# Eight accumulating transfers from GpSimd's queue in the fourth batch of a pooled attention with a mixture of experts

## Chip, cores and metric

One core of a Trainium2 chip runs the whole program. The metric is the device time of one execution in microseconds; less is better.

## What is computed

Attention with pooled queries over 8 batches of 8 heads, then a mixture of experts in which each row goes to one of 8 experts. Cut to what matters here:

```python
# q, k, v: (8, 8, 1152, 64) float32
q_pool = q.reshape(B, H, S // 2, 2, D).mean(axis=3)
scores = scale * np.matmul(q_pool, k.transpose(0, 1, 3, 2))
scores = scores - np.max(scores, axis=-1, keepdims=True)
attn = np.exp(scores)
attn = attn / (np.sum(attn, axis=-1, keepdims=True) + 1e-09)
x = np.matmul(attn, v)                      # -> (4608, 512)
# each row of x: the expert of the largest logit, relu(x @ w1[e]) @ w2[e], times its weight
```

## The kernel before

**Tiling.** The attention goes batch by batch (`b` from 0 to 7), in a batch by pairs of heads (`hp` from 0 to 3), and in a pair by halves of the 576 pooled queries (`half`, 288 each). Such a half of a pair is called a half pair below; there are 64 of them, counted from 0, and 24 to 31 are the fourth batch (`b == 3`). The transposed scores of a half pair fill one score tile `s` of 128 partitions by 9 chunks by 2 heads by 288 queries, that is 5184 floats in each partition. There are four such tiles (`UNITS`), so half pair 33 takes the tile that 29 had.

**What is done with a half pair.** `scores` lets TensorE multiply keys and queries chunk by chunk into a PSUM bank (L631). VectorE scales each chunk into `s` and takes its minimum (L635), nine of these "takes" a half pair. Then a bound for the exponential is spread to all partitions (L656, L662), and ScalarE overwrites `s` with exponentials in five pieces (L666). `chunk_sum` lets GpSimd add the nine chunks up: a first fold of chunks 0 to 2 with 3 to 5 and a second that adds 6 to 8 (both 1728 floats a partition), and a third of 576 (all L726), into a tile `fold` of which there are three; TensorE adds up the partitions of the folds of both halves (L716). In the last half pair of a batch only the first fold is made (L722), and TensorE does the rest (L709). `values` multiplies `s` with the value tile (L770), nine steps a half pair, about ten microseconds after the exponentials.

**GpSimd's other work in a batch.** It adds neighbouring queries before their transposition (`qp`, L520, four a batch), which VectorE then turns (`qT`, L533), and it issues six scatters into the lists of the experts (L951).

**The order** of each engine's instructions is fixed before the run. `Flow.add` takes each step with an engine, an estimated time, a key (a due time; lower goes first) and what it waits for; `Flow.emit` plays the steps through with these estimates and puts each engine's instructions in the order in which the play started them. `Flow.carry` adds a step that issues a transfer, and behind it a step on a pretended engine (`DMA2` where GpSimd issues) for the transfer's own time. A step holds the tiles in its `holds` from the first step that names a tile to the last, in the play and on the chip. The play's figures that matter here are these:

```python
LATE = dict(PE=250, DVE=130, ACT=130, POOL=60, SP=100, DMA=1700, DMA2=1700, REST=0)
return s and self.add("DMA2" if eng == "POOL" else "DMA", move, lambda: None, key, [s], holds, late=late + (1200 if eng == "POOL" else 0))
def pool(n):
    return 140 + 2.125 * n
```

GpSimd executes in order: an instruction that waits holds up all behind it.

Of the kernel before, what the change touches and what calls it, by code (L numbers as in the profile page):

```python
# [9 lines left out]
F32 = mybir.dt.float32  # L10
# [4 lines left out]
ALU = mybir.AluOpType  # L15
# [22 lines left out]
K_SUM = 25  # L38
# [12 lines left out]
RAW = 6  # L51
XT = 2
LI_BUFS = 6
RE_BUFS = 8
LEAD = 100
AHEAD = 190
XR2 = 4
XR = 6
Y_BUFS = 2
# [204 lines left out]
def kernel(  # L264
# [10 lines left out]
    nc = tc.nc  # L275
# [4 lines left out]
    P = 128  # L280
# [7 lines left out]
    NFC = DF // P  # L288
# [128 lines left out]
    class Pools:  # L417
        h = last = None
# [20 lines left out]
    def act(n):  # L439
        return 110 + 0.833 * n  # L440

    def dve(n):
        return 67 + 1.042 * n
# [12 lines left out]
    def hold_of(kind, make):  # L456
        h = Hold(kind, lambda: make(h))
        return h
# [7 lines left out]
    def score_banks(o):  # L466
        return hold_of("st", lambda h: o.ps_s.tile([P, 2, 512], F32, **h.own("st")))

    def value_banks(o):
        return hold_of("pa", lambda h: o.ps_m.tile([P, 2, 512], F32, **h.own("pa", 1)))  # L470

    def done(*steps):
        return [s for s in steps if s is not None]
# [219 lines left out]
    def every(steps):  # L693
        return [*{id(s): s for s in steps if s is not None}.values()]
# [62 lines left out]
    def values(o, f, key, x, s, ready, hp, half, xT):  # L757
        pa = value_banks(o)
        key += K_AV
        to = slice(half * HQ, (half + 1) * HQ)  # L760
        p = None
        for c in range(NC):
            mark = Pools()

            def product(c=c, mark=mark):

                for i in range(2):
                    for h in range(2):
                        up, cs = slice(i * D, (i + 1) * D), slice(h * D, (h + 1) * D)
                        mark.made = nc.tensor.matmul(pa.t[cs, i, :HQ], x.vn.t[up, h, c, :], s.t[up, c, h],  # L770
                                                     start=c == 0, stop=c == NC - 1, tile_position=(up.start, cs.start))

            p = f.add("PE", 485, product, key + 20.0 * c / NC, done(p, x.v, ready[c]), [pa, x.vn, s], QUADS)
            mark.step = p
            o.marks.append(mark)
        a = f.add("ACT", act(HQ) - 44, lambda: nc.scalar.copy(xT.t[:, hp, to], pa.t[:, 0, :HQ]), key + 20 + K_FREE, done(p), [pa, xT])
        return f.add("DVE", 100 + dve(HQ), lambda: nc.vector.tensor_tensor(  # L777
            xT.t[:, hp, to], xT.t[:, hp, to], pa.t[:, 1, :HQ], ALU.add), key + 20 + K_FREE, done(p, a), [pa, xT])
# [25 lines left out]
    def attend(o, f, key, b, hp, xT, sm, summed):  # L804
        x = load_pair(o, f, key, b, hp)
        outs = []
        end = not o.exact and hp == NHP - 1 and b == B - 1
        for half in range(2):
            at = key + 20 * half
            s, r = scores(o, f, at, x, half, EXPS)  # L810
            summed += chunk_sum(o, f, at + 20, s, r, b, hp, half, sm, summed[-1:])
            outs.append(values(o, f, at + 10 - (40 if end and half else 0), x, s, r, hp, half, xT))
        return done(*outs)

# [401 lines left out]
    def add_raw(m, cm, reuse):  # L1216
        m.r = cm.enter_context(tc.tile_pool(name="mr", bufs=RAW, reuse_waits=reuse))

    def add_moe(m, cm, reuse, **side):
        m.x = cm.enter_context(tc.tile_pool(name="mx", bufs=1, reuse_waits=reuse, **side))  # L1220
        m.w = cm.enter_context(tc.tile_pool(name="mw", bufs=1, reuse_waits=reuse, **side))
        m.w1 = [cm.enter_context(tc.tile_pool(name=f"mw1{j}", bufs=1, reuse_waits=reuse, **side)) for j in range(4)]
        m.ps = cm.enter_context(tc.tile_pool(name="mps", bufs=2, space=PSUM, reuse_waits=reuse))
# [182 lines left out]
    with ExitStack() as cm, ExitStack() as units, ExitStack() as pairs:  # L1406
        o, m = open_attention(False, cm, pairs, units), Pools()
        m.stored = []

        def swap_units():  # L1410
            units.close()
            add_moe(m, units, "tile", side="right")

        f = Flow(dict(st=S_BUFS, s=UNITS, qn=1, vn=3, kp=2, qp=1, kT=KT_BUFS, qT=KT_BUFS,
                      fold=FOLD_BUFS, pa=1, sm=2, xT=2, rec=2, row=ROW_BUFS, lw=1, ex=1, de=1,
                      ohb=1, di=2, re=2, rec2=RE_BUFS, li=LI_BUFS, ix=LI_BUFS, xr=XR, xq=XR2, xt=XT, raw=RAW, x=1, x0=1, **{f"{w}{j}": 1 for w in ("w1", "w2") for j in range(4)}, **{f"h{c}": 1 for c in range(NFC)}, ph=2, py=2, px=2, y=Y_BUFS),
                 ("vn", "fold", "s", "st"), ("x", "xt", "xq", *(f"{w}{j}" for w in ("w1", "w2") for j in range(4)), *(f"h{c}" for c in range(NFC)), "ph", "py", "px", "y"), swap_units)
        hold = []
        pw = score_banks(o)

        def warm_up():
            for i in range(WARM):
                nc.tensor.matmul(pw.t[:, 0], ones, ones.unsqueeze(1).broadcast_to([P, 4, P]), start=True, stop=True)

        if WARM:
            f.add("PE", 2900 * WARM, warm_up, -1000, holds=[pw])
        for b in range(B):
            xT = tile_of(o, "xT", [P, NHP, NQ])
            rec = tile_of(o, "rec", [QP, 2, 3, H])
            sm = tile_of(o, "sm", [P, HQ], bufs=1)  # L1430
            outs, summed = [], []
            for hp in range(NHP):
                outs += attend(o, f, PAIR * (b * NHP + hp), b, hp, xT, sm, summed)
                if b == hp == 0:
                    o.gate = f.carry("SP", 2700, gate_weights, 60, outs, [], 900)
                    f.carry("SP", 960, empty_lists, 1, outs, [], 900)
                    f.carry("SP", 2000, last_rows, 100, outs, [], 3400)
            key = PAIR * (b * NHP + NHP)
            outs.append(row_sums(o, f, key, sm, done(*summed), rec, b == B - 1))
            if b == B - 1:  # L1440
                for x in first:
                    x.rows = x.rows()
                    hold += x.rows
            outs = routing(o, f, key, b, xT, rec, outs, hold)
            if b == B - 2:
                hold, first = first_slots(o, m, f, key + K_FIRST, outs)


        def swap_pairs():
            pairs.close()  # L1450
            add_raw(m, pairs, "tile")
            m.x0 = pairs.enter_context(tc.tile_pool(name="mx0", bufs=1, reuse_waits="tile"))

        raw_here = done(f.add("SP", 10, swap_pairs, key - 1000, o.turned))
        table = slot_table(o, f, key + K_SLOT + K_TAB, outs[:1])
        flag(o, f, key + K_SLOT + 20, [*outs, *table])
        order = [(early, i, TW) for i in range(EARLY)] + [(wide, i, TW) for i in range(WIDE)]
        order += [((etab, rtab), i, T) for i in range(STATIC_SLOTS)]
        base, marks = key + K_SLOT, []
        for i, (tab, s, n) in enumerate(order):  # L1460
            at = base + SLOT * i
            experts, places_ = tab if isinstance(tab, tuple) else (tab[:, 0], tab[:, 1])
            if tab is early:
                x = first[s]
                known = done(x.found)
            else:
                x = tokens_of(o, f, at - AHEAD, places_, s, n, table, outs, m=m, steps=marks[i - 2],
                              used=PLACES[s] if tab is wide else BU)
                known = table
            weights_of(m, f, x, at - 200 if i else at - 1000, experts, s, [*known, *raw_here])  # L1470
            turn_tokens(o, m, f, x, at - (110 if i == 0 else 50), i == 0, raw_here)
            x.w1, x.w1_ready = split_weights(m, f, x, "w1", at - 40, 8, 0)
            first_products(o, m, f, x, at)
            x.w2, x.w2_ready = split_weights(m, f, x, "w2", at, 10, 0)
            second_products(o, m, f, x, at + 50)
            marks.append(() if f.room is None or i < 2 else x.marks)
        f.add("POOL", 2500, lambda: nc.gpsimd.drain(), at - AHEAD + 4, x.rows)
        f.emit()
        by_hand.close()
# [4 lines left out]
    with tc.If(more > 0):  # L1484
        again = nc.values_load(stab[0:1, 1:2], min_val=0, max_val=1,
                               skip_runtime_bounds_check_because="a comparison's result")
        with tc.If(again > 0):
            reset_state()
            empty_lists()
            with ExitStack() as cm:  # L1490
                o = open_attention(True, cm, cm, cm)
                with tc.For_i(0, B, 1) as b:
                    f = Flow()
# [14 lines left out]
        with ExitStack() as cm:  # L1508
            o, m, f = Pools(), Pools(), Flow()
# [5 lines left out]
            with tc.For_i(first, last, 1) as s:  # L1515
                x = tokens_of(o, f, 0, rtab, s, T, (), ())
# [34 lines left out]
```

## Time and profile before

| | us |
|---|---|
| median of 3 runs | 1131.37 (1130.13 to 1131.44) |
| the profiled execution, whole | 1125.42 |
| its span, first instruction to last | 1123.6 |
| attention in it, roughly | 0 to 660 |
| mixture of experts in it, roughly | 660 to 1123.6 |

In what follows PE is TensorE's matmul, PEld its weight load, DVE VectorE, ACT ScalarE, POOL GpSimd and SP SyncE. Times within the program count from the start of the span.

### The profile page before, as it was taken

The page shows a single profiled execution, that of the slowest core. Times are in us where ns is not written, and L with a number is a line of the kernel's source. Part 1 is how long each engine was busy: PE and PEld are TensorE (multiplying, and loading weights), DVE is VectorE, ACT ScalarE, POOL GpSimd, SP SyncE. Part 2 cuts the span into 40 slices and gives each one's busy share as a digit, 9 for nine tenths or more (in the row PEclk, how much of TensorE's full clock was granted, in tenths as well). Part 3 has the DMA queues.
Part 4 walks back from the last instruction along what each step waited for, and adds up shares of the span by engine and source line. Part 5 has one row for each costly group of instructions (what it writes and reads, how often), then busy time and mean ns, then how long its engine had stood idle before and what let it go on. Part 6 is the DMA issues. An engine that isn't in the chain of part 4 may idle for free.

```text
span 1123.6 us, 32966 instructions
## 1 busy us (share of the span) xinstructions
PE 1109.8 (99%) x13317; PEld 797.1 (71%) x13317; DVE 875.9 (78%) x2244; ACT 619.7 (55%) x835; POOL 857.6 (76%) x488
## 2 busy tenths in 40 slices
PE   9999999999999999999999999999999999999997
PEld 5565565565565565655655558998889989899996
DVE  7898998988989979989989969755555665677761
ACT  3756565666556656566557465544444445555551
POOL 3899999999999899998999854576666655456511
PEclk9999999999999999999999999999999999999999
DMA  9876757537738738637635159865555666577640
GB/s 158 141 139 111 129 86 124 113 66 122 115 66 132 112 64 139 114 66 134 112 63 99 27 169 243 232 188 166 164 174 176 201 192 191 191 233 255 229 158 30
DMA packets 387502, 158.06 MB, mean 141 GB/s; under 512 B 302694, under 2 KB 357762, under 8 KB 387342
## 3 DMA queue, kind: packets, MB, share of 16 engines
q1 hardware_dynamic: 376718, 134.91, 54.4%
q0 software_dynamic: 10464, 20.78, 5.9%
q8 instruction: 106, 1.74, 0.8%
q14 instruction: 54, 0.44, 0.2%
q10 hardware_dynamic: 160, 0.20, 0.1%
HBM read 135.02 MB, written 22.07 MB: 140 GB/s over the span
## 4 chain that ended last, share of the span: by engine, by line
PE 66%; DVE 15%; issue 6%; POOL 5%; DMA 4%; SPq 2%; ACT 0%; POOLq 0%; DVEq 0%; ACTq 0%
PE py L1384 17%; PE ph L1354 16%; PE pa L770 15%; PE st L631 14%; DVE s L635 8%; POOL fold L726 3%; DMA vn<-in_v_dram 2%; SPq L490 2%; DVE kT L529 2%; PE st L716 2%; DVE row L937 1%; PE st L709 1%; POOL qp L520 1%; DVE qT L533 1%; DMA x_runs<-row 1%
## 5 line engine op out<-in xcount | busy, mean ns | idle before, releaser
L666 ACT ACTIVATE s<-s,bias 128x1152 f32<-128x1152 f32 (+1 forms) x320 | 351.3, 1152 | 166.4 <-DVE bias L662 156.7
L635 DVE TENSOR_SCALAR_CACHE_REDUCE s<-st 128x576 f32<-128x576 f32 x576 | 415.1, 748 | 32.4 <-PE st L631 21.7
L631 PE MATMUL st<-qT,kT 64*64 64x288 f32 x4608 | 359.9, 407 | 4.6 <-DVE s L635 2.8
L770 PE MATMUL pa<-s,vn 64*64 64x288 f32 x4608 | 351.4, 404 | 1.0 <-DVE xT L777 0.8
L631 PEld LDWEIGHTS st<-qT,kT 64*64 64x64 f32 x4608 | 166.9, 133 | 121.3 <-DVE s L635 37.3
L770 PEld LDWEIGHTS pa<-s,vn 64*64 64x64 f32 x4608 | 174.6, 133 | 104.3 <-DVE xT L777 10.8
L726 POOL TENSOR_TENSOR fold<-s 128x1728 f32<-128x1728 f32 x55 | 213.0, 3875 | 5.5 <-ACT s L666 3.1
L726 POOL TENSOR_TENSOR fold<-fold,s 128x1728 f32<-128x1728 f32 x55 | 213.0, 3876 | 0.9
L1354 PE MATMUL ph<-xh,w1h 128*128 128x248 f32 (+4 forms) x512 | 155.6, 304 | 0.2 <-DVE hl L1364 0.2
L1354 PE MATMUL ph<-xh,w1l 128*128 128x248 f32 (+4 forms) x512 | 154.6, 302 | 0.0
L1354 PE MATMUL ph<-xl,w1h 128*128 128x248 f32 (+4 forms) x512 | 154.6, 302 | 0.0
L1226 DVE TENSOR_TENSOR w2l<-raw,w2h 128x1024 fp32r<-128x1024 f32 x64 | 78.3, 1223 | 80.6 <-ACT w2h L1311 76.8
L1083 POOL DMA_INDIRECT xr<-x_runs,ix x76 | 97.5, 1283 | 51.6 <-issue 26.0
L1384 PE MATMUL py<-w2h,hh 128*128 128x512 f32 x328 | 128.1, 391 | 0.0
L1384 PE MATMUL py<-w2h,hl 128*128 128x512 f32 x328 | 127.8, 390 | 0.0
L1384 PE MATMUL py<-w2l,hh 128*128 128x512 f32 x328 | 127.8, 390 | 0.0
L1393 POOL DMA_INDIRECT out_dram<-y,rec x41 | 43.9, 1071 | 85.7 <-ACT y L1401 70.3
L1362 ACT ACTIVATE hh<-ph 128x372 fp32r<-128x372 f32 (+4 forms) x100 | 49.3, 493 | 108.2 <-PE ph L1354 108.0
L1354 PEld LDWEIGHTS ph<-xh,w1h 128*128 128x128 f32 x512 | 96.4, 188 | 2.6 <-issue 0.9
L1354 PEld LDWEIGHTS ph<-xl,w1h 128*128 128x128 f32 x512 | 96.4, 188 | 0.7
L1354 PEld LDWEIGHTS ph<-xh,w1l 128*128 128x128 f32 x512 | 96.4, 188 | 0.0
L1364 DVE SCALAR_TENSOR_TENSOR hl<-ph,hh 128x372 fp32r<-128x372 f32 (+4 forms) x100 | 55.6, 556 | 51.1 <-ACT hh L1362 50.8
(230 smaller groups left out, 1339.1 us busy)
## 6 DMA issues: line engine op xcount, KB each, us to landing
raw<-in_moe_w_dram SPq DMA_DIRECT2D x128, 512.0 KB
kp<-in_k_dram SPq DMA_DIRECT2D x124, 144.0 KB
vn<-in_v_dram SPq DMA_DIRECT2D x124, 144.0 KB
qn<-in_q_dram SPq DMA_DIRECT2D x120, 144.0 KB
x_runs<-row SPq DMA_DIRECT2D x96, 99.0 KB
xr<-x_runs,ix POOLq DMA_INDIRECT x76, 4.3
x_runs<-empty SPq DMA_DIRECT2D x4, 297.0 KB
xq<-x_runs,ix POOLq DMA_INDIRECT x52, 3.3
```

What stands on the lines that cost most here:

```text
L631: nc.tensor.matmul(pt.t[to, h, :HQ], x.kT.t[up, c * P + i * D:c * P + (i + 1) * D], x.qT.t[up, cols], start=True, stop=True, tile_position ...
L635: nc.vector.tensor_scalar(s.t[:, c], pt.t[:, :, :HQ], -SCALE, None, op0=ALU.mult, op1=ALU.min, accum_out=mx.t[:, c:c + 1],)
L666: nc.scalar.activation(s.t[:, c0:c0 + n], s.t[:, c0:c0 + n], AF.Exp, bias=bias.t, scale=-1.0)
L726: add = lambda to, a, b: nc.gpsimd.tensor_tensor(to, a, b, ALU.add)
L770: mark.made = nc.tensor.matmul(pa.t[cs, i, :HQ], x.vn.t[up, h, c, :], s.t[up, c, h], start=c == 0, stop=c == NC - 1, tile_position=(up.sta ...
L1083: ins = nc.gpsimd.indirect_dma_start(out=x.xr[i // NQD].t[:, i % NQD, :], out_offset=None, in_=xg, in_offset=bass.IndirectOffsetOnAxis(ap= ...
L1226: (nc.gpsimd if eng == "POOL" else nc.vector).tensor_tensor(lo, raw, hi.bitcast(F32), ALU.subtract)
L1354: mark.made = nc.tensor.matmul(view()[:, i, :], a[:, c, fp], b[:, c, :n], start=c == 0 and k == 0, stop=c == NDC - 1 and k == 2)
L1362: a = f.add("ACT", act(nb * n) - 44, lambda home=home, apart=apart: nc.scalar.activation(home(0), apart(), AF.Relu), at - 20, done(p), [ph ...
L1364: d = f.add("DVE", dve(nb * n), lambda home=home, apart=apart: nc.vector.scalar_tensor_tensor(home(1), apart(), 0.0, home(0).bitcast(F32), ...
L1384: mark.made = nc.tensor.matmul(py.t, blocks(a)[:, c * x.nr + r], b[:, c % 2, :], start=c == 0 and k == 0, stop=c == NFC - 1 and k == 2)
L1393: ins = nc.gpsimd.indirect_dma_start(out=out, out_offset=bass.IndirectOffsetOnAxis(ap=x.re.t.bitcast(I32)[:, r, 0:1], axis=0), in_=y.t, in ...
```

## The change

A tile `probe` of 128 partitions by 1728 floats is added, and GpSimd sets it to zero once, at the start. In the fourth batch each half pair gets one more step on GpSimd: a transfer that adds the last `n` floats of each partition of the score tile, after the exponentials, onto the first `n` of `probe`. `n` is 1728 for both halves of the first two pairs, 1152 for those of the third and 576 for those of the fourth: 864, 864, 576 and 288 KB a transfer. Nothing reads `probe`. Each transfer waits for the exponentials of its half pair and for the landing of the transfer before it, holds the score tile, and enters the play with 1200 ns for its issue and 6000 ns for its move. Its key is that of the half pair's folds.

```diff
             summed += chunk_sum(o, f, at + 20, s, r, b, hp, half, sm, summed[-1:])
+            if not o.exact and b == 3:
+                n = (1728, 1728, 1152, 576)[hp]
+                o.joined = f.carry("POOL", 1200, lambda n=n, s=s: o.join(n, s), at + 20 + K_SUM, done(o.joined, *every(r)), [s, o.onto], 6000)
             outs.append(values(o, f, at + 10 - (40 if end and half else 0), x, s, r, hp, half, xT))
...
-                      ... ph=2, py=2, px=2, y=Y_BUFS),
-                 ("vn", "fold", "s", "st"), ("x", "xt", ...), swap_units)
+                      ... ph=2, py=2, px=2, y=Y_BUFS, probe=1),
+                 ("vn", "fold", "s", "st", "probe"), ("x", "xt", ...), swap_units)
...
+        onto = hold_of("probe", lambda h: o.ld.tile([P, 1728], F32, name="probe", bufs=1))
+        flat = lambda t: t.rearrange("p c h n -> p (c h n)")
+
+        def join(n, s):
+            nc.gpsimd.dma_start(out=onto.t[:, :n], in_=flat(s.t)[:, -n:], accum_op=ALU.add)
+
+        o.join, o.onto = join, onto
+        o.joined = f.add("POOL", 1800, lambda: nc.gpsimd.memset(onto.t, 0.0), -999, holds=[onto])
```

## Rows read from the trace of the kernel before

**Rows 1.** The page: busy time of each engine, and GpSimd's and the DMA's slices.

```profile
PE 1109.8 (99%) x13317; PEld 797.1 (71%) x13317; DVE 875.9 (78%) x2244; ACT 619.7 (55%) x835; POOL 857.6 (76%) x488
POOL 3899999999999899998999854576666655456511
DMA  9876757537738738637635159865555666577640
```

**Rows 2.** Windows, one a batch from the fourth on, the last one cut short.

```profile
core 0: us, PE busy (x) PEld busy (x) DVE busy (x) ACT busy (x) POOL busy (x), PEclk, DMA share, GB/s
260.10:341.50 81.40, 81.07 (x1332) 48.63 (x1328) 73.39 (x221) 48.98 (x65) 78.50 (x33) 1.00 0.62 105
341.50:423.90 82.40, 81.86 (x1340) 48.64 (x1336) 73.68 (x221) 49.18 (x65) 78.58 (x33) 1.00 0.64 103
423.90:505.10 81.20, 81.03 (x1332) 48.53 (x1328) 73.31 (x221) 49.06 (x65) 78.46 (x33) 1.00 0.61 105
505.10:587.60 82.50, 81.83 (x1340) 48.60 (x1336) 73.66 (x221) 49.14 (x65) 78.56 (x33) 1.00 0.61 103
587.60:640.00 52.40, 51.95 (x845) 30.03 (x841) 48.81 (x178) 26.68 (x42) 48.48 (x22) 1.00 0.37 72
```

**Rows 3.** Groups by line, GpSimd alone, in 260.1 to 341.5.

```profile
L520 POOL TENSOR_TENSOR qp<-qn 128x576 f32<-128x576 f32 x4 | 5.6, 1404 | 1.6 <-ACT s L666 1.6
L951 POOL DMA_INDIRECT lists<-re,di x6 | 5.5, 923 | 1.0 <-issue 0.7 <-DVE s L635 0.2 <-PE st L656 0.2
```

**Rows 4.** Groups by line, GpSimd alone, whole span: other issues, and settings of a tile.

```profile
L1047 POOL DMA_DIRECT2D li<-lists x13 | 9.4, 722 | 0.3 <-issue 0.2
L1058 POOL DMA_INDIRECT xr<-x_runs,rec x6 | 9.7, 1620 | 12.6 <-PE pa L770 11.5 <-issue 0.6 <-PE ph L1354 0.3
L359 POOL MEMSET empty<- 128x132 f32 x1 | 0.2, 208 | 0.1
```

**Rows 5.** The DMA view: queues, and a GpSimd issue with its time to landing.

```profile
q1 hardware_dynamic: 376718, 134.91, 54.4%
q0 software_dynamic: 10464, 20.78, 5.9%
li<-lists POOLq DMA_DIRECT2D x7, 8.0 KB, 2.7
```

**Rows 6.** GpSimd's timeline: its start, and 317 to 336.

```profile
17.09 0.79 POOL L520 TENSOR_TENSOR qp<-qn 128x288 f32<-128x288 f32 x1 [12.85 <-DMA qn<-in_q_dram]
...
317.15 3.89 POOL L726 TENSOR_TENSOR fold<-s 128x1728 f32<-128x1728 f32 x1
...
322.14 3.87 POOL L726 TENSOR_TENSOR fold<-fold,s 128x1728 f32<-128x1728 f32 x1
...
335.00 1.40 POOL L520 TENSOR_TENSOR qp<-qn 128x576 f32<-128x576 f32 x1
```

**Rows 7.** L666, L770 and L635 from 0 to 312.5, 329.4 and 333.95: durations, first and last starts.

```profile
L666 ACT ACTIVATE s<-s,bias x150: 757/1241/1260, 18.9 to 311.6; 128x1152 f32<-128x1152 f32 x120, 128x576 f32<-128x576 f32 x30
L770 PE MATMUL pa<-s,vn x2160: 402/402/454, 20.9 to 328.9; 64*64 64x288 f32 x197
L635 DVE TENSOR_SCALAR_CACHE_REDUCE s<-st x298: 714/753/759, 8.4 to 333.9; 128x576 f32<-128x576 f32 x149
```

**Rows 8.** VectorE's waits in 260 to 342 (waiter, releaser, total, times, longest), and its timeline.

```profile
DVE s L635 <- PE st L631: 2.3, 9, 0.7
DVE qT L533 <- POOL qp L520: 0.9, 1, 0.9
...
333.93 0.76 DVE L635 TENSOR_SCALAR_CACHE_REDUCE s<-st 128x576 f32<-128x576 f32 x1 [0.76 <-PE st L656]
```

**Rows 9.** Chain of waits in 230 to 380: a stretch of it, in order of time.

```profile
249.76 3.86 POOL fold L726
253.62 1.38 POOL qp L520
255.02 0.84 DVE qT L533 x2
```

More of the change, by code (lines that the diff above doesn't have):

```diff
@@ L1415 @@
                       fold=FOLD_BUFS, pa=1, sm=2, xT=2, rec=2, row=ROW_BUFS, lw=1, ex=1, de=1,
-                      ohb=1, di=2, re=2, rec2=RE_BUFS, li=LI_BUFS, ix=LI_BUFS, xr=XR, xq=XR2, xt=XT, raw=RAW, x=1, x0=1, **{f"{w}{j}": 1 for w in ("w1", "w2") for j in range(4)}, **{f"h{c}": 1 for c in range(NFC)}, ph=2, py=2, px=2, y=Y_BUFS),
-                 ("vn", "fold", "s", "st"), ("x", "xt", "xq", *(f"{w}{j}" for w in ("w1", "w2") for j in range(4)), *(f"h{c}" for c in range(NFC)), "ph", "py", "px", "y"), swap_units)
+                      ohb=1, di=2, re=2, rec2=RE_BUFS, li=LI_BUFS, ix=LI_BUFS, xr=XR, xq=XR2, xt=XT, raw=RAW, x=1, x0=1, **{f"{w}{j}": 1 for w in ("w1", "w2") for j in range(4)}, **{f"h{c}": 1 for c in range(NFC)}, ph=2, py=2, px=2, y=Y_BUFS, probe=1),
+                 ("vn", "fold", "s", "st", "probe"), ("x", "xt", "xq", *(f"{w}{j}" for w in ("w1", "w2") for j in range(4)), *(f"h{c}" for c in range(NFC)), "ph", "py", "px", "y"), swap_units)
         hold = []
```

## Prediction, made before the changed kernel ran

> **What bounds the kernel now.** I read the page first, for the engines and the slices of GpSimd [rows 1]. The reader is to see that GpSimd's 76% is a mean over two stages: nearly every slice of the attention has a 9 or an 8, and in the experts' stage there are 4 to 6. The change sits in the attention, so I cut the windows by batch [rows 2]. The fourth batch lasts 81.4 us; TensorE is busy for 81.1 of it, GpSimd for 78.5, VectorE for 73.4. TensorE ends the program, but GpSimd has just 2.9 us left, and 3.8, 2.7, 3.9 and 3.9 in the windows behind it. Its groups in that batch say what these 2.9 are [rows 3]: 1.6 are a wait ahead of one addition of queries and 1.0 are six short gaps of 0.17 ahead of the scatters, which every issue has and which nothing can use. So about 1.6 to 1.9 us of a batch is free on GpSimd. VectorE's waits [rows 8] name TensorE, and GpSimd once in this batch, for 0.9 us; no transfer is among the releasers there, so the loads aren't late now. The chain of waits shows the same place one batch earlier [rows 9]: two steps of GpSimd in a row, then VectorE's turn of the queries. GpSimd is thus a second bound, just behind TensorE.
>
> **The change part by part.**
>
> *The zeroing.* One setting of 128 by 1728 floats at the start. The 132-column one took 0.21 us [rows 4]; by columns that is 2.7 us at most. GpSimd sat idle for 12.85 us ahead of its first addition of queries at 17.09 [rows 6], so the zeroing costs nothing; without that cover it would cost these 2.7.
>
> *The issues.* Eight transfers are issued by GpSimd. The trace has none that accumulates. The nearest in place is the scatter in the same batch: 0.92 us each, with its gap 1.09 [rows 3]. The plain issue of 128 partitions took 0.72, and the dearest gather 1.62, with the gap 1.79 [rows 4]. An issue that does less than nothing isn't possible. I take 1.09, since the scatters run beside the same work: 8 x 1.09 = 8.7 us, bounds 8 x 0.72 = 5.8 and 8 x 1.79 = 14.3. Against 1.6 free, GpSimd ends the fourth batch some 7 us behind (4 to 13). The later windows give back about 2 to 3 us each beyond the gaps, so that debt is gone only in the seventh batch. Being behind isn't yet lost time: what counts is who waits for GpSimd.
>
> *The transfers themselves.* The DMA view gives two prices [rows 5]. The queue of GpSimd held its packets for 5.9% of 16 engines' 1123.6 us, or 1061 us of one engine, for 20.78 MB: 51 us a MB. The load queue: 54.4%, or 9780 us, for 134.91 MB: 72 us a MB. A full transfer is 0.885 MB, so 2.8 to 4.0 us over 16 engines if bytes are moved once. An addition must read what it adds to, so I double that as the estimate: 5.6 to 8.0 us; for the 1152-float ones (0.590 MB) 3.8 to 5.3. To this comes the time to landing of a small issue, 2.7 us. A full one therefore lands about 8 to 11 us after its issue, a 1152-float one 6.5 to 8.0.
>
> The Trainium skill says of the additions made in the DMA engines (Collectives: The Full Stack, "The bandwidth ceiling: the fold count and why AG ≠ RS ≠ AR") that they run at half the rate of a copy because two sources are read. No row here shows it; by its 31 GB/s an engine for a copy a full transfer would be 3.6 us of data, and the forecast below would be some 2 us lower. The sum doesn't use that figure.
>
> All eight are 5.31 MB, 17 us of all engines at the low price and 48 at the high one doubled, of 81.4. The DMA share of that batch, 0.62 [rows 2], would go to 0.83 at least. The loads get slower. They have room, as rows 8 show, so I cost that at nothing in the forecast and leave the high end to a rival below.
>
> *What waits.* (a) Each issue also waits for the landing of the one before it; queued behind it on GpSimd are the folds and the addition of queries. Half pairs come every 81.4 / 8 = 10.2 us, so at 8 to 11 us the predecessor has mostly landed and this costs about nothing. (b) The score tile is now held until the transfer has read it. Take half pair 29, the tightest of the eight. Its last exponential started at 311.6 (150 of them are 30 half pairs of five), its second fold ended at 322.14 + 3.87 = 326.0, its last value product started at 328.9 (2160 are 30 x 72), and VectorE's first take into the same tile, for half pair 33, was at 333.93 (the 298th is 33 x 9 + 1) [rows 6, 7, 8]. In the code the new step has the key of the folds and stands behind them, so I put the issue behind the second fold. Five earlier issues, 5 x 1.09 - 1.6 = 3.9 us, move that end to 329.9; the transfer lands 2.7 + 3.8 = 6.5 us later, at 336.4, and the take is 2.5 us late. Low end: the issue slips in ahead of the second fold, 3.9 us earlier, and nothing is late. High end: 326.0 + (5 x 1.79 - 1.6) + 2.7 + 5.3 = 341.4, 7.5 us late. In the play the tile is held even longer, 1.2 + 0.06 + 6 + 1.2 + 1.7 = 10.2 us from the start of the issue, so the scores of half pairs 32 to 35 will be planned later by some microseconds and value products put in front of them. (c) The addition of queries at 335.0 [rows 6] feeds the turn for which VectorE already waited 0.9 us [rows 8]. Its key comes after the folds of half pair 30, so the debt moves it too; about 7 us of debt there meet the same late scores of (b), and don't add to them.
>
> *The sum.* A late take stops VectorE, then TensorE's score products. TensorE has nothing to catch it up with: by the windows it is idle for 0.2 to 0.7 us a batch [rows 2]. So the 2.5 us stay: on the profiled execution 1125.4 + 2.5 = 1127.9, which stood 6.0 below the median; on the median 1131.4 + 2.5 = **1133.9**. Other half pairs of the eight are late at the same time or less, and the lateness of one is that of all behind it, so they aren't added.
>
> **The rivals.**
>
> *Absorbed.* Values are computed long after the exponentials (311.6 against a last product at 328.9), so TensorE holds a stock of ready value products and can do them while the scores wait; VectorE has 8 us a batch to catch up [rows 2]. For it: that stock. Against it: one bank for the value products, and the wait of VectorE for the queries [rows 8]. Time: 0 to 2.2 more, about 1132.
>
> *Transfers too slow.* If a full one takes longer than the 10.2 us of a half pair, the wait (a) becomes the price: GpSimd stands still with folds and queries behind it. At four times the load price it would be 2.7 + 4 x 4.0 = 18.7 us, four waits of 8.5 each, less the 333.9 - 326.0 = 7.9 of room for the folds: 26 more, 1157. At 14 us it is 4 x 3.8 - 7.9 = 7 more. The 864 KB beside loads at a share of 0.62 speak for it, the price of the queues against it. The Trainium skill's rule that each DMA engine goes round its queues packet by packet (DMA: Bandwidth & Descriptors, "Queues, rings and completion order") would make it likelier, as large packets would alternate with the loads' small ones; no row here shows it. Time 1141 to 1160.
>
> *A luckier order.* Every order behind the fourth batch is made anew. The four full windows differ, 81.2 to 82.5, mean 81.9 [rows 2]; if the new order made all four like the best, 4 x 0.7 = 2.7 less, 1128.7. Nothing in the change aims there. This is the side on which the kernel gets faster: 1127.4 to 1129.1.
>
> That the change doesn't do what it says, because the transfers wait for their turn until long after the batch, is part of the first rival: the chain then lies beside the work.
>
> **How the numbers follow.** GpSimd's debt reaches the score tiles, 2.3 to 10 more (10 is the whole 8.7 with the high move): 0.40. Absorbed: 0.36. Too slow: 0.12. Luckier: 0.12. The likeliest gives 1133.9. The range leaves out the luckier case and the upper half of the slow one: 1129.5 to 1146. Some 0.2% (2.3 us) is what a measurement of this kernel can tell from no change: faster 0.12, same 0.36, slower 0.52.
>
> **What would show it.** Right: eight issues of about 0.9 us between 260 and 350; GpSimd's additions of queries at 335 some 5 to 7 us later; a wait of a take in half pairs 32 to 35 for a transfer or for TensorE, 2 to 3 us; from 400 on a constant shift of the takes. Wrong: issues above 1.6 us, or an idle GpSimd ahead of them that a transfer ends (the slow rival); no shift of the takes at 406 (absorbed); a shift that grows after the fifth batch, which my sum has no term for.

## The result and the profile after

| | us |
|---|---|
| before, median of 5 runs beside those of after | 1131.37 (1129.10 to 1132.57) |
| after, median of 5 runs | 1137.57 (1135.03 to 1140.18) |
| ratio | 1.0058, 95% interval 1.0042 to 1.0073 |
| after, the profiled execution and its span | 1135.03 and 1133.5 |

The change costs 0.58%, or 6.6 us (4.8 to 8.3). The spans differ by 9.9, but the profiled execution of before stood 6.0 below its own median, that of after only 2.5 below, so 3.5 of the 9.9 are not the change's.

The page of after (busy time of each engine, the DMA's slices, and the queues with packets, MB and share of 16 engines' span), against [rows 1, 5]:

```profile
PE 1114.7 (98%) x13317; PEld 796.3 (70%) x13317; DVE 878.6 (78%) x2244; ACT 620.1 (55%) x835; POOL 867.6 (77%) x497
DMA  8876767549888647746635148955556655677640
q1 hardware_dynamic: 376718, 134.91, 54.8%
q0 software_dynamic: 11616, 26.08, 8.4%
```

The windows of after, one a batch as in [rows 2] (length, busy time and records of each engine, clock, DMA share, GB/s):

```profile
260.10:341.50 81.40, 80.27 (x1300) 45.54 (x1296) 70.63 (x213) 48.01 (x64) 77.85 (x38) 1.00 0.90 153
341.50:423.90 82.40, 79.81 (x1280) 47.71 (x1282) 71.87 (x217) 46.24 (x63) 75.68 (x33) 1.00 0.66 111
423.90:505.10 81.20, 80.23 (x1316) 47.51 (x1312) 73.32 (x218) 47.72 (x64) 80.00 (x34) 1.00 0.64 105
505.10:587.60 82.50, 81.58 (x1332) 48.10 (x1325) 73.23 (x219) 49.10 (x65) 78.92 (x32) 1.00 0.60 103
```

GpSimd's queue moved 5.30 MB more, and the DMA share of the fourth batch went from 0.62 to 0.90. What isn't obvious: GpSimd is busy for *less* time in the fourth and fifth windows than before (77.85 and 75.68 against 78.50 and 78.58) although it has eight more issues. An engine with more to do and less busy time is waiting. TensorE starts fewer matmuls there, 1300 and 1280 in place of 1332 and 1340: its work comes later.

The groups by tile of after (min, median and max duration in ns, first and last start), and its waits: VectorE's in 260 to 342, as in [rows 8], then GpSimd's in 255 to 430:

```profile
L1432 POOL DMA_DIRECT2D probe<-s x8: 862/1018/1613, 262.0 to 350.2; - x8
L1435 POOL MEMSET probe<- x1: 1528/1528/1528, 4.2 to 4.2; 128x1728 f32 x1
DVE s L635 <- PE st L631: 3.3, 5, 1.7
DVE qT L533 <- POOL qp L520: 0.5, 1, 0.5
POOL qp L520 <- DMA qn<-in_q_dram: 5.5, 1, 5.5
POOL fold L726 <- ACT s L666: 2.5, 2, 2.1
```

No engine waits for one of the eight transfers: VectorE's takes name TensorE, as before. Instead GpSimd waits 5.5 us for a load of queries, `qn`. Whether that wait is the transfers' doing is looked at below.

I also followed each half pair: the end of its last value product (L770) in after, less the same in before. It is 0.1 earlier at half pair 25, 2.7 earlier at 34, then 2.1 later at 35, 5.3 at 36 and 6.3 at 44. So TensorE first does value products that were ready while the scores are late, and pays from half pair 35 on. (e1 below, which has the new order and no transfer, shows the same: 0.8 to 3.2 earlier at half pairs 29 to 34, 1.7 later at 35. It is the new order's doing.) The difference of this shift between half pairs 25 and 44 is called the **net shift** below, 6.3 us here; it takes out how an execution started, and stands beside each time. It comes from one execution of each kernel. It lies within 1.8 us of what the runs give, but for e8 (2.8 below) and e2 (4.6 above), so a difference of a microsecond or two in it alone shows little.

### The profile page after: what moved, and what is told of

Read it like the earlier page. It is cut to its first block, busy times and chain, and to the rows that moved or that the text cites. A ratio compares the mean times of both kernels' runs of the same rounds, so it can differ in the third digit from the quotient of the medians.

```text
span 1133.5 us, 32967 instructions
## 1 busy us (share of the span) xinstructions
PE 1114.7 (98%) x13317; PEld 796.3 (70%) x13317; DVE 878.6 (78%) x2244; ACT 620.1 (55%) x835; POOL 867.6 (77%) x497
## 4 chain that ended last, share of the span: by engine, by line
PE 68%; DVE 13%; issue 7%; POOL 6%; SPq 3%; DMA 2%; ACT 1%; POOLq 0%; DVEq 0%; ACTq 0%
PE py L1387 17%; PE ph L1357 16%; PE pa L770 16%; PE st L631 15%; DVE s L635 7%; POOL fold L726 4%; SPq L490 2%; PE st L716 2%; DMA qn<-in_q_dram 1%; DVE row L940 1%; PE st L709 1%; DVE kT L529 1%; POOL qp L520 1%; PE st L656 1%; DVE qT L533 1%
## 5 line engine op out<-in xcount | busy, mean ns | idle before, releaser
L666 ACT ACTIVATE s<-s,bias 128x1152 f32<-128x1152 f32 (+1 forms) x320 | 350.9, 1151 | 177.6 <-DVE bias L662 162.4
L635 DVE TENSOR_SCALAR_CACHE_REDUCE s<-st 128x576 f32<-128x576 f32 x576 | 415.2, 749 | 37.2 <-PE st L631 27.8
L770 PE MATMUL pa<-s,vn 64*64 64x288 f32 x4608 | 350.4, 404 | 2.5 <-DVE xT L777 2.1
L770 PEld LDWEIGHTS pa<-s,vn 64*64 64x64 f32 x4608 | 175.6, 133 | 103.4 <-DVE xT L777 13.6
L726 POOL TENSOR_TENSOR fold<-s 128x1728 f32<-128x1728 f32 x55 | 215.7, 3924 | 8.1 <-ACT s L666 6.0
L726 POOL TENSOR_TENSOR fold<-fold,s 128x1728 f32<-128x1728 f32 x55 | 215.8, 3926 | 1.0
L1086 POOL DMA_INDIRECT xr<-x_runs,ix x76 | 90.9, 1197 | 50.0 <-issue 26.1
L1086 POOL DMA_INDIRECT xq<-x_runs,ix x52 | 60.7, 1168 | 46.9 <-PE py L1387 21.2
```

The costliest lines, as they stand in the source:

```text
L635: nc.vector.tensor_scalar(s.t[:, c], pt.t[:, :, :HQ], -SCALE, None, op0=ALU.mult, op1=ALU.min, accum_out=mx.t[:, c:c + 1],)
L666: nc.scalar.activation(s.t[:, c0:c0 + n], s.t[:, c0:c0 + n], AF.Exp, bias=bias.t, scale=-1.0)
L726: add = lambda to, a, b: nc.gpsimd.tensor_tensor(to, a, b, ALU.add)
L1086: ins = nc.gpsimd.indirect_dma_start(out=x.xr[i // NQD].t[:, i % NQD, :], out_offset=None, in_=xg, in_offset=bass.IndirectOffsetOnAxis(ap= ...
```

## Experiments

Ratios are to runs of the kernel before beside each kernel, as its median differed between the series (1131.4, 1129.8, 1123.6, 1123.3). "Changed order" is that of after on every engine, "old order" that of before; in the old order, the transfers are issued right behind the second fold of their half pair (the first in the last half pair of the batch), and the play knows nothing of them. All keep the zeroing unless said.

| kernel | order | the eight transfers | us over before (95%) | net shift |
|---|---|---|---|---|
| after | changed | accumulating, full size | +6.6 (4.8 to 8.3) | 6.3 |
| e1_order_only | changed | none | +1.2 (-0.2 to 2.8) | 1.3 |
| e4_small | changed | accumulating, 8 KB | +4.1 (2.4 to 5.8) | 4.1 |
| e9_after_own_source | changed | accumulating, no score tile held | +6.5 (4.6 to 8.3) | 5.2 |
| e7_plain_copy | changed | plain copies, full size | +2.9 (1.8 to 3.9) | 1.1 |
| e8_memset | changed | a fill of 1100 floats each | +7.2 (5.6 to 8.7) | 4.4 |
| e3_no_move | a third | accumulating, full size | +4.3 (2.9 to 5.6) | 4.9 |
| e2_beside_play | old | accumulating, full size | +9.7 (7.7 to 11.6) | 14.3 |
| e5_beside_small | old | accumulating, 8 KB | +4.5 (2.9 to 6.1) | 4.0 |
| e6_own_source | old | accumulating, no score tile held | +11.8 (10.1 to 13.6) | 10.7 |
| e11_beside_plain | old | plain copies, full size | +7.3 (5.8 to 8.8) | 7.1 |
| e10_batch7 | old | six, in the last batch | +0.9 (-0.1 to 1.8) | -0.5, ahead of its transfers; 0.8 from half pair 55 to 63 |

### Order or transfers: e1, e4, e2, e3

```diff
 # e1_order_only
-            nc.gpsimd.dma_start(out=onto.t[:, :n], in_=flat(s.t)[:, -n:], accum_op=ALU.add)
+            pass
 # e4_small
-                n = (1728, 1728, 1152, 576)[hp]
+                n = 16
 # e2_beside_play: no step in the play; in chunk_sum, for b == 3, in the step of the second fold
+                add(u.t, u.t, s.t[:, 6:9])
+                o.join((1728, 1728, 1152, 576)[hp], s)
 # e3_no_move: the play sees the issue, not the transfer's 6000 ns
-                o.joined = f.carry("POOL", 1200, lambda ..., [s, o.onto], 6000)
+                o.joined = f.add("POOL", 1200, lambda ..., [s, o.onto])
```

Expected of e1: 

> The order of every engine is that of the changed kernel, and the eight transfers are left out; the zeroing stays. Theory A (the order): the changed kernel is 6.2 us slower because the play, which holds each score tile 10.2 us from the issue, puts the scores of half pairs 32 to 35 later; this run then keeps most of it, 4 to 7 us above before (1135 to 1138). Theory B (the transfers themselves: eight issues of about 1 us on GpSimd and tiles that come free late): this run is within 2 us of before (1130 to 1133). My recorded sum was of kind B, with 2.5 us from late tiles.

Expected of e2: 

> The order of every engine is that of the kernel before; the same eight transfers are issued right behind the second fold of each half pair (behind the only fold in the last), and the play knows nothing of them. Theory A (the order): within 2 us of before (1130 to 1133). Theory B (the transfers): 5 to 8 us above before (1136 to 1139), since the order leaves no room and each late tile stops VectorE in order; by my own sum of late tiles 2.5 us (1134).

Expected of e3: 

> The eight transfers are issued as in the change, but the play has no step for their move: it plans 1.2 us of GpSimd for each and lets the score tile go when the issue ends. Theory A (the planned hold makes the order): 0 to 3 us above before (1131 to 1134), so half or less of the loss. Theory B (the transfers): 5 to 8 above (1136 to 1139), as the hardware waits stay.

Expected of e4: 

> The order and the issues are those of the changed kernel, but each transfer adds 16 floats a partition, 8 KB in all, in place of up to 864 KB. It lands in some 3 us, so no tile comes free late. Theory A (the order) and the share of B that is issue time: as the changed kernel, 1136 to 1139. The share of B that is bytes (late tiles, slowed loads): 2 to 4 us faster than the changed kernel, 1133 to 1135.

The order alone costs 1.2 us, not clear of nothing. Eight tiny transfers in it cost 4.1, the full ones 6.6. So the chain is about 1.2 for the order (1.5 either way), 2.9 for the issues and 2.5 for the bytes (2.4 or so either way, being differences of two measurements). Left in the old order the same transfers cost 9.7: the new order saves some 3 us rather than costing them. e3, whose play knows the issues alone, stands at 4.3, between what its two theories gave; with intervals this wide it is not shown to be better than after. e2, and below e5, e6 and e8, came out dearer than the expectation nearest to them (9.7 against 5 to 8, 4.5 against 2 to 4, 11.8 against 8 to 10, 7.2 against 3 to 4.5).

In e2 the cause looked plain. Its VectorE waits in 285 to 345 (us in total, times, longest):

```profile
DVE s L635 <- DMA probe<-s: 10.7, 4, 4.1
DVE s L635 <- PE st L631: 3.2, 8, 1.2
```

Four takes wait for a transfer to let go of its score tile, which is what the prediction had in mind. e6 was made to test it.

### How the bytes act: e5, e6, e9

```diff
 # e6_own_source (from e2) and e9_after_own_source (from after)
-            nc.gpsimd.dma_start(out=onto.t[:, :n], in_=flat(s.t)[:, -n:], accum_op=ALU.add)
+            nc.gpsimd.dma_start(out=onto.t[:, :n], in_=onto.t[:, :n], accum_op=ALU.add)
 # e5_beside_small (from e2): both issues with 16 in place of 576 to 1728
```

Expected of e5: 

> Every engine keeps the order of the kernel before; GpSimd issues one accumulating transfer right behind the same folds as in the run that left the order alone, but of 16 floats a row (8 KB) in place of 2304 to 6912 bytes a row. That run stood 9.7 us above before. If what it lost was the bytes (a score tile held for the transfer, loads made slower), most goes: +2 to +4 us, the price that small transfers had in the changed order (4.1 with an order worth 1.2), and VectorE's takes wait for no transfer. If the loss is that GpSimd's 8 us of issues stand in an order that was not planned for them, it stays at +7 to +10, with the takes late by GpSimd's folds.

Expected of e6: 

> The order of the kernel before, the eight transfers of full size behind the same folds, but each reads the accumulator itself (zeros) in place of the exponentials, so no score tile waits for a transfer; issues and bytes are the same (what is added is zero either way not the exponentials: the accumulator's content differs, and nothing reads it). The run that read the exponentials stood 9.7 us above before. If the held score tile is what carried the transfers' length to TensorE, this falls to +3 to +6 (issues, and loads that share the DMA engines). If slower loads and GpSimd's own time carried it, it stays at +8 to +10.

Expected of e9: 

> The changed kernel in its own order, the eight accumulating transfers reading the accumulator itself in place of the exponentials: same issues, same bytes, but no score tile has to wait for a transfer (the accumulator's content differs, and nothing reads it). In the order of before, taking the held tile away saved nothing. If the held tile costs nothing here either, as VectorE's waits say, the time stays at that of the changed kernel, +5 to +8 us. If the late take of the prediction is hidden behind other waits, 2 to 3 us go: +3 to +4.

The held tile is not the main thing. Without it e6 costs 11.8, no less than e2, and in the changed order e9 costs 6.5 beside after's 6.6; each difference is good to 2.6 either way. By the net shift e6 stands 3.6 below e2 and e9 1.1 below after, so a smaller price of the hold isn't excluded. e5 says that in the old order it is the bytes all the same: 4.5 without them. What they do stands in the timelines (start, duration, engine, line, and in brackets the idle time ahead with its releaser). First SyncE's load issues and GpSimd in e6, then the same of e5:

```profile
267.70 7.76 SPq L490 DMA_DIRECT2D kp<-in_k_dram  x4
283.53 7.20 SPq L490 DMA_DIRECT2D qn<-in_q_dram  x4
293.36 1.41 POOL L520 TENSOR_TENSOR qp<-qn 128x576 f32<-128x576 f32 x1 [7.66 <-DVE re L914]
345.98 2.13 POOL L520 TENSOR_TENSOR qp<-qn 128x576 f32<-128x576 f32 x1
```

```profile
267.18 3.91 SPq L490 DMA_DIRECT2D kp<-in_k_dram  x4
277.67 4.21 SPq L490 DMA_DIRECT2D qn<-in_q_dram  x4
284.97 1.49 POOL L520 TENSOR_TENSOR qp<-qn 128x576 f32<-128x576 f32 x1
337.73 2.12 POOL L520 TENSOR_TENSOR qp<-qn 128x576 f32<-128x576 f32 x1
```

With full transfers beside them the four issues of a `kp` load take 7.76 us in place of 3.91 (5.15 in before), and the four of the `qn` load behind it start 5.9 later and take 7.20 in place of 4.21. GpSimd stands still for 7.66 us ahead of the addition that needs `qn` (the releaser named there, a small instruction of VectorE, is the last event on record, but that addition reads `qn` alone, and VectorE had let go of `qp` at 285.60). e2 shows the same idle time ended by the load itself:

```profile
295.00 1.40 POOL L520 TENSOR_TENSOR qp<-qn 128x576 f32<-128x576 f32 x1 [8.21 <-DMA qn<-in_q_dram]
```

In all four kernels with an idle time there the addition starts 2.6 to 3.5 us after the last issue of its load: 290.73 and 293.36 in e6, 291.80 and 295.00 in e2, 285.71 and 289.25 in e11, 283.28 and 286.77 in before. So it is the load in each. GpSimd has next to no slack, so the wait reaches the addition of queries that before had at 335.00 [rows 6], and there the turn and the scores behind it. The shift of TensorE follows that of this one instruction, within 1.4 us, in all four kernels of the old order that have the transfers in this batch:

| kernel | `qp` of before's 335.00 | later by | last value product of half pair 30 later by |
|---|---|---|---|
| e5_beside_small | 337.73 | 2.7 | 4.1 |
| e11_beside_plain | 340.61 | 5.6 | 5.3 |
| e6_own_source | 345.98 | 11.0 | 11.4 |
| e2_beside_play | 347.61 | 12.6 | 13.0 |

In the changed order the play has moved that addition ahead, so it is only 0.4 later in after (335.38). There the loss comes at the last `qp` of the next batch, and again it is one instruction that TensorE follows, in all six kernels of that order:

| kernel | start of that `qp` | later than in e1 | last value product of half pair 44, later than in e1 |
|---|---|---|---|
| e7_plain_copy | 380.80 | -0.7 | -1.1 |
| e1_order_only | 381.51 | | |
| e4_small | 383.17 | 1.7 | 1.5 |
| e8_memset | 383.47 | 2.0 | 1.5 |
| e9_after_own_source | 384.04 | 2.5 | 2.1 |
| after | 385.96 | 4.5 | 4.3 |

It waits for `qn` (5.50 us in after, 4.15 in e4; in e1 VectorE's turn of the queries before it, which ends at 381.43, comes last), but here the bytes aren't shown to be why the load is late. By the packet records the last of the eight transfers of after had landed at 357.0, 18 us before that load was issued, and e8, which moves nothing, waits longer. GpSimd and SyncE's loads in after, then the same of e8:

```profile
354.90 2.14 POOL L520 TENSOR_TENSOR qp<-qn 128x576 f32<-128x576 f32 x1
357.07 4.44 SPq L490 DMA_DIRECT2D qn<-in_q_dram  x4
375.34 4.39 SPq L490 DMA_DIRECT2D qn<-in_q_dram  x4
385.96 1.41 POOL L520 TENSOR_TENSOR qp<-qn 128x576 f32<-128x576 f32 x1 [5.50 <-DMA qn<-in_q_dram]
```

```profile
353.17 1.40 POOL L520 TENSOR_TENSOR qp<-qn 128x576 f32<-128x576 f32 x1
354.60 4.44 SPq L490 DMA_DIRECT2D qn<-in_q_dram  x4
371.76 4.59 SPq L490 DMA_DIRECT2D qn<-in_q_dram  x4
383.47 1.41 POOL L520 TENSOR_TENSOR qp<-qn 128x576 f32<-128x576 f32 x1 [5.64 <-DMA qn<-in_q_dram]
```

There is one buffer for `qn`. In all six kernels the earlier load starts 0.02 to 0.03 us after the end of the `qp` that had to read the buffer first, and the later one 17.1 to 18.3 us after that, behind SyncE's other issues. So a GpSimd that is behind gets its own loads late, with or without bytes: from e1 to after the first of these `qp` starts 3.0 later (351.88 and 354.90) and the last 4.5. What the bytes add in this order, 2.5 by the runs and 2.2 by the net shift above e4, is thus not traced to one wait.

### GpSimd's time, and the addition: e7, e11, e8

```diff
 # e7_plain_copy (from after) and e11_beside_plain (from e2)
-            nc.gpsimd.dma_start(out=onto.t[:, :n], in_=flat(s.t)[:, -n:], accum_op=ALU.add)
+            nc.gpsimd.dma_start(out=onto.t[:, :n], in_=flat(s.t)[:, -n:])
 # e8_memset (from after)
+            nc.gpsimd.memset(onto.t[:, :1100], 0.0)
```

Expected of e7: 

> The changed kernel in its own order, with plain copies in place of accumulating transfers: the same rows, read once and written, nothing added (the accumulator's content differs, and nothing reads it). If the addition makes a row slow (a 6912-byte row took 553 to 712 ns on its engine), rows take 250 to 400 ns, a full transfer lands 4 to 5.5 us after its issue in place of 7.1 to 7.5, the DMA share in the fourth batch falls from 0.89 toward 0.75, and of the 2.3 to 2.5 us that the bytes cost above small transfers about half goes: 1133.5 to 1136. If the rows take as long without the addition, the time stays at that of the changed kernel, +6 to +7 us.

Expected of e11: 

> The order of before on every engine and the eight transfers behind the same folds of the fourth batch, as plain copies of the exponentials in place of accumulations (the accumulator's content differs, and nothing reads it). Issues took 0.56 to 0.62 us without accumulating and 0.86 to 1.6 with it, and a 6912-byte row 267 to 350 ns on its engine in place of 553 to 712. If loads made late by the transfers' engine time are what the bytes cost (a wait of GpSimd for qn of 7 to 8 us in the accumulating run), that wait shrinks below 4 us and the run stands +2 to +5 us above before in place of +9.7. If the issues and the held tile carry it, it stays at +7 or more.

Expected of e8: 

> The changed kernel's order on every engine, with a fill of 1100 floats a row of the accumulator in place of each transfer: about 1 us of GpSimd's time each (the fill of 1728 took 1.53), no DMA at all. Without the transfers the order alone stood 1.2 us above before, with transfers of 8 KB 4.1. If an issue costs as GpSimd's time, this is +3 to +4.5 as with the small transfers. If it is the queue (the descriptors written, the transfer's completion, loads issued beside it), the fill costs little: +1 to +2.

The groups of the tile in e7 and e8:

```profile
L1432 POOL DMA_DIRECT2D probe<-s x8: 557/578/617, 262.3 to 348.0; - x8
```

```profile
L1432 POOL MEMSET probe<- x8: 1004/1006/1021, 261.7 to 348.4; 128x1100 f32 x8
```

Plain copies of the same bytes cost the changed order 2.9 in place of 6.6, or by the net shift nothing (1.1 beside 1.3 of the order alone). Two things are smaller there at once: an issue holds GpSimd for 0.58 us in place of 1.02, and the transfer loads the DMA engines less (their share in 260 to 342 is 0.84, where I expected it to fall toward 0.75). By the packet records a row of 6912 bytes took a median of 267, 280, 288 and 348 ns on its engine in the four full copies of e7, and 552, 560, 538 and 535 in those of after: about twice, as the Trainium skill's half rate has it (Collectives: The Full Stack, "The bandwidth ceiling: the fold count and why AG ≠ RS ≠ AR"). The figure there, 31 GB/s an engine for a copy, is 25.9 here (6912 bytes in 267 ns), and 12.5 with the addition (in 552 ns). No run separates the two things. GpSimd's time alone would go with the net shift: at the prices of an issue below, and 1.0 us a fill, e7, e4 and e8 put 4.5, 6.8 and 8.0 us on GpSimd and shift by -0.2, 2.8 and 3.1 more than e1, so 4.0 to 4.9 us would have been free in each. That is an estimate.

In the old order plain copies don't save as much: e11 stands at 7.3, where my expectation was 2 to 5 if the late loads were the price, and 7 or more if the issues and the held tile were. Its GpSimd waited 5.02 us for `qn`, in place of 7.66 to 8.21, so the load is late beside plain copies too. One take of VectorE waits for a transfer besides; no run has plain copies without the hold, so what that costs is open:

```profile
DVE s L635 <- DMA probe<-s: 5.5, 1, 5.5
```

GpSimd of e11:

```profile
263.56 3.87 POOL L731 TENSOR_TENSOR fold<-fold,s 128x1728 f32<-128x1728 f32 x1
289.25 1.41 POOL L520 TENSOR_TENSOR qp<-qn 128x576 f32<-128x576 f32 x1 [5.02 <-DVE s L635]
340.61 1.41 POOL L520 TENSOR_TENSOR qp<-qn 128x576 f32<-128x576 f32 x1
```

These rows also give the net price of an issue. From that fold to the `qp` seven issues lie between; the stretch is 340.61 - 263.56 - 5.02 = 72.0 us. In e5 (its fold started at 263.67 and nothing but the gaps ahead of the scatters is waited for) it is 74.1. In before it is 335.00 - 265.36 - 1.55 = 68.1, by [rows 6] and these rows:

```profile
265.36 3.89 POOL L726 TENSOR_TENSOR fold<-fold,s 128x1728 f32<-128x1728 f32 x1
286.77 1.41 POOL L520 TENSOR_TENSOR qp<-qn 128x576 f32<-128x576 f32 x1 [1.55 <-ACT s L666]
```

So a plain issue costs GpSimd 0.56 us, and an accumulating one 0.85 (tiny ones; longer gaps at the scatters behind them are in it): 6.8 for eight. e8 replaces them by fills of 1.0 us and has no DMA at all. By the net shift it is beside the tiny transfers (4.4 and 4.1); by its runs it is dearer (7.2, 5.6 to 8.7, against 2.4 to 5.8). So an issue isn't shown to cost more than the same GpSimd time spent otherwise. By the runs the fills, without a byte moved, cost no less than the whole change (7.2 and 6.6); why they come out dearer in the runs than in the trace stays open.

### Another place: e10

```diff
 # e10_batch7 (from e2)
-                if b == 3:
+                if b == 7:
```

Expected of e10: 

> The order of before on every engine, with the transfers in the last batch in place of the fourth, behind the same second folds: six of them (four full, two of 1152 floats; the last pair of that batch has no such folds). There the trace of before shows GpSimd busy 67.7 of 83.0 us and the DMA engines 0.39, against 79.1 of 82.0 and 0.62 in the fourth batch. If the price is GpSimd time without slack and loads made late, most of it goes: 0 to +3 us. If it is the transfers' own length (the score tile held, the doubled traffic), six of eight keep three quarters of the 9.7 us that the same placing cost in the fourth batch: +6 to +8.

The window of the last batch in before, and then in e10 with the group of its transfers:

```profile
587.00:670.00 83.00, 82.22 (x1305) 47.46 (x1301) 67.79 (x227) 46.62 (x65) 67.65 (x31) 1.00 0.39 96
```

```profile
587.00:670.00 83.00, 81.58 (x1290) 46.91 (x1286) 66.83 (x223) 47.80 (x66) 69.84 (x37) 1.00 0.67 149
L1443 POOL DMA_DIRECT2D probe<-s x6: 867/962/1270, 593.1 to 652.1; - x6
```

Six of the eight transfers with the same issues, 4.7 of the 5.3 MB, cost 0.9 us, not clear of nothing, where GpSimd has 15 us left and the DMA engines were at 0.39. All eight, placed alike in the fourth batch, cost 9.7. The price is the place's. Which part of the place makes it, GpSimd's slack, the idle DMA engines or the lack of another batch's loads behind it, this run doesn't separate.

## Why the prediction was right, and where it was wrong

**Direction and range.** Slower, inside the range, at 6.6 us where 2.5 were forecast. That it lay in the range was luck: the term that carried the whole sum, the late take, did not occur, and two terms that I set at nothing, or only into a debt, made up the loss.

**GpSimd as the second bound**: right, and the base of all that follows. e5, with 8 KB a transfer, loses 4.5 us; e8, with none, loses 6.0 more than e1 by the runs and 3.1 by the net shift; e10 loses 0.9 where GpSimd is free.

**The zeroing**: right; 1.53 us at 4.2, inside the idle start.

**The issues**: 8.7 us forecast; 8 x 0.85 = 6.8 measured, inside the bounds of 5.8 to 14.3. The gap of 0.17 us that I counted with each issue stands ahead of the scatters alone; the new issues have none. The step that failed is what was made of the debt. I had it meet the late scores of (b) and add nothing; with 8 KB moved, so with nothing held for long, it costs 2.9 us over the order.

**The transfers**: forecast 8 to 11 us to landing for a full one; by the packet records 7.4, 7.1, 7.5 and, with 1.0 MB of loads between issue and landing (0.3 to 0.6 beside the others), 10.4. The 1152-float ones landed in 6.5 and 7.8 (forecast 6.5 to 8.0). Doubling for the addition was right for the rows, as e7 shows. GpSimd's queue held 8.4% of 16 engines' 1133.5 us, less the 1061 us of before: 462 us for 5.3 MB, 87 us a MB against the doubled 102 to 144. The remark that the forecast would be some 2 us lower by the 31 GB/s of the Trainium skill (Collectives: The Full Stack, the same section) doesn't fit the sum, which uses a 1152-float transfer: 2.4 us by that figure, an estimate, in place of 3.8, so 1.4 lower.

**The loads**: the step that failed most in the old order. "They have room, as rows 8 show, so I cost that at nothing." Those rows say that no *VectorE* step waited for a load. The load that matters is `qn`, which has one buffer and is read by GpSimd, and a wait of 1.6 us ahead of a `qp` stood in [rows 3]; I left it there as put down to ScalarE, whose tile that addition doesn't read. Late loads are 7.3 of the 11.8 us of e6 (what it stands above e5, whose GpSimd has no such wait). In after the load is late too, but it is late in e8 without any transfer, and the 2.5 us that after stands above e4 aren't shown to be its price.

**(a) the wait for the transfer before**: right in after, no such wait; e3, which planned no time for the transfer, has one of 2.4 us, and a take of VectorE that waits 3.5 us for a transfer.

**(b) the held score tile**, the 2.5 us of the sum: wrong. The sixth transfer was issued at 329.55 and had landed at 337.37, near the 329.9 and 336.4 of the working. The take was the mistake: I took 333.93 from the old order and didn't move it, though I had written that the play would plan these scores later. The first take of half pair 33 in after, then in e1, which has no transfer:

```profile
339.87 0.75 DVE L635 TENSOR_SCALAR_CACHE_REDUCE s<-st 128x576 f32<-128x576 f32 x1
```

```profile
339.37 0.75 DVE L635 TENSOR_SCALAR_CACHE_REDUCE s<-st 128x576 f32<-128x576 f32 x1
```

The order alone moves it 5.4 us, past the landing, so nothing waits; and e9, without the hold, saves 0.1 by the runs. In the old order VectorE does wait for it (e2), where GpSimd, behind by its own wait for `qn`, had issued late as well; without the hold most of that time is lost elsewhere (e6).

**(c) the `qp` at 335.0, 5 to 7 us later**: wrong in after (0.4), as the new order put it ahead; later where the order was left (2.7 to 12.6), and there the time follows it. In after the same kind of wait, a late `qp` with the turn and the scores behind it, stands one batch on, 4.5 later than in e1; it did add, where I had said that it would not.

**The rivals.** Absorbed: no. Half pairs 29 to 34 end their values 0.3 to 2.7 us early, but e1 does the same without transfers, and the stock that TensorE spent there is paid for at 35 to 39. Too slow: its price was not reached, and GpSimd never waits for a transfer in after. But loads beside the transfers do get slower, as the issues of e6 show. The Trainium skill's packet turn (DMA: Bandwidth & Descriptors, "Queues, rings and completion order") would be in line with that; no run here separates it from a mere lack of DMA time. Luckier order: no, 1.2 dearer if anything.

**A shift that grows after the fifth batch**, which I had no term for, is there: after goes from 6.3 at half pair 44 to 8.2 at 53. All six kernels of the changed order grow by 1.4 to 1.9 between these two, e1 without any transfer too, and those of the old order by 0.4 or less. It is the order's, not the transfers'.

## What to carry to other kernels

Ask of each engine near its limit what *it* waits for, and look for the load with one buffer that it reads. In the old order extra DMA traffic cost where that load came late, more than where the new transfer was waited for; and an engine that falls behind frees that buffer late, and so makes its next load late itself. A wait that a profile shows for a new transfer needn't be its price; take the hold away before believing it. Before you take a time from the old kernel's trace into a forecast, ask whether the new order moves it. Side work of GpSimd's queue belongs in a stage where GpSimd and the DMA engines have slack: eight such transfers cost 9.7 us in one batch and six of them 0.9 in another.

## What the hardware showed beyond this

Behind an accumulating issue GpSimd's own records grow, with 8 KB as with 864, and those behind plain copies don't. In after:

```profile
261.95 1.00 POOL L1432 DMA_DIRECT2D probe<-s  x1
262.65 4.22 POOL L726 TENSOR_TENSOR fold<-fold,s 128x1728 f32<-128x1728 f32 x1
266.48 1.75 POOL L520 TENSOR_TENSOR qp<-qn 128x576 f32<-128x576 f32 x1
```

The fold's record is 4.22 us where 3.87 is usual [rows 6], and the `qp` 1.75 where it took 1.40, yet the next start comes after 3.83 us as ever. The records overlap, and the issue seems dearer by its record (1.00 us) than from start to start (0.70). With each further issue they grow, to 1.61 us for the last issue; after an idle time they are short again. For what such an issue takes of GpSimd's time, go by starts, not by durations. But the longer record counts for whoever waits for its end: the load of `qn` at 357.07 starts when the `qp` of 354.90 ends its 2.14 us (the rows of after above), as in e8 it starts when one of 1.40 us ends.
